# The first pair of heads through GpSimd's casting queue, and the last tile stored in two transfers per queue

## The chip, the core and the metric

The kernel runs on one core of a Trainium2 chip. The metric is the device time of one execution in microseconds (us); for the kernel before it is 431.96, the median of three runs (430.53 to 432.34). The profile is of one execution of the same program, and its span, from the first to the last instruction, is 430.6 us. Engines are called as in the profile: PE is TensorE's matmuls, PEld its weight loads, DVE is VectorE, ACT is ScalarE, POOL is GpSimd, SP is SyncE. A "q" behind an engine's name is its instruction sequencer, which among other things issues transfers.

## What is computed

Attention with a squared ReLU in place of the softmax, for 8 batches of 12 heads, 448 positions and 64 channels a head; its output, with the heads side by side, goes through a gated feed-forward block (768 to 1536 and back).

```python
def _attn_ref(q, k, v):                      # q, k, v: (8, 12, 448, 64) fp32
    scores = scale * np.matmul(q, k.transpose(0, 1, 3, 2))
    attn = np.maximum(scores, 0.0) ** 2 / S
    return np.matmul(attn, v)

def _moe_ref(x, w_gate, w_val, w_out):       # x: (3584, 768), d_ff = 1536
    g = x @ w_gate
    gelu = 0.5 * g * (1.0 + erf(g * inv_sqrt2))
    val = x @ w_val
    return (gelu * val @ w_out)              # (3584, 768) fp32
```

## The kernel before

All matmuls are in bf16. The inputs are fp32, so nearly all loads are issued on GpSimd's queue, whose transfers cast on the way. The kernel makes a list of operations for each engine, estimates when each could start, and emits them in that order (`run_plan`). Where it expects TensorE to wait within the first 30 us, it puts dummy matmuls (`fill`, on a tile of zeros named `warm`), so that the engine stays busy.

The beginning: a warm-up of dummy matmuls, then for each pair of heads of batch 0 the transposes of q and k on TensorE, a copy of them out of PSUM by VectorE, the scores (TensorE), the ReLU (ScalarE), the square (VectorE), and the product with v (TensorE, `add_values`).

```python
warm_op = Op("PE0", 3.8, lambda: emit_warm_up())
...
def emit_warm_up():
    t = new_bank(None)
    for _ in range(9):
        for j in range(2):
            nc.tensor.matmul(t[HALF[j], :], warm[:, HALF[j]], warm[:, :],
                             start=True, stop=True, tile_position=(0, P * j))
```

The first two heads of batch 0 are loaded in another way than the rest: SyncE issues two fp32 transfers, one for q and one for k, into a tile `first`. VectorE then rounds the first head of both to bf16, and ScalarE the second.

```python
def load_first():
    first = const.tile([128, 2, SC * D], f32)
    got = []
    for i, src in enumerate((q, k)):
        op = Op("SP", 0.0, lambda i=i, src=src: nc.sync.dma_start(
            first[HALF[i], :, :], src[0, 0:2].rearrange("h (p c) d -> p h (c d)", c=SC)), prio=-1)
        ...
    def emit(j):
        ...
        if j:
            nc.scalar.copy(o, first[:, j, :])
        else:
            nc.vector.tensor_copy(o, first[:, j, :])
...
got = load_first()
for h0, h1 in ((2, 4), (4, 8), (8, 12)):
    load_qk(0, 0, h0, h1)            # GpSimd's queue, casting
    load_qk(0, 1, h0, h1)
    if h0 == 2:
        POOL[0].after = got[1]
        POOL.append(Op("POOL", 0.6, lambda: make_identity(nc, ident)))
    if h0 > 2:
        load_v(0, h0 - 4, h1 - 4)
```

The transposes of a pair, and the place in the order that its product with v is given (`step` is the planned time of one unit of scores):

```python
for c in range(SC):                          # 7 chunks x 2 heads = 14 transposes a pair
    for j in range(2):
        nc.tensor.transpose(t[HALF[j], c, :], src[:, 2 * (2 * m + r) + j, c, :],
                            ident[:, :], tile_position=(0, P * j))
...
x = lo + u * step + max(4.5, (3.2 + 2 * (pr == 0) if b == 0 else 2.5) * step)
```

The end: the output is made in tiles of 128 rows (two chunks of 64) and in column groups, 0 to 383 and 384 to 767. The last tile has three groups, 0 to 383, 384 to 575 and 576 to 767, so that the last piece is small. Each group has 24 pairs of matmuls, then a copy out of PSUM, which VectorE does for the last tile. In the last tile each group is stored as soon as it is copied: one half of the rows by SyncE's queue and the other half by ScalarE's.

```python
bounds = (0, OGS, OGS + OGS // 2, 2 * OGS) if last else (0, OGS, 2 * OGS)   # OGS = 384
cols = slice(bounds[g], bounds[g + 1])
...
cp = Op("DVE" if last else "ACT", 0.48, emit_copy, [ops[1][-1]], prio=1)
if last:
    SP.append(Op("SP", 0.6, lambda: emit_store(0, nc.sync, cols), [cp], prio=-1))
    ACT.append(Op("ACT", 0.1, lambda: emit_store(1, nc.scalar, cols), [cp], prio=-1))
elif g == NG - 1:
    SP.extend(Op("SP", 0.6, lambda j=j: emit_store(j, nc.sync, slice(0, d_model)), [cp], prio=-1)
              for j in range(2))
```

Of the kernel before, what the change touches and what calls it, by code (L numbers as in the profile page):

```python
# [88 lines left out]
def kernel(  # L89
# [10 lines left out]
    nc = tc.nc  # L100
    f32 = mybir.dt.float32
    bf16 = mybir.dt.bfloat16
# [3 lines left out]
    B, H, S, D = q.shape  # L106
    P = 64
    SC = S // P
# [10 lines left out]
    NG = 2  # L119
# [9 lines left out]
    const = ctx.enter_context(tc.tile_pool(name="const", bufs=1))  # L129
    wpool = ctx.enter_context(tc.tile_pool(name="wpool", bufs=1))  # L130
    qkv = ctx.enter_context(tc.tile_pool(name="qkv", bufs=2))
# [21 lines left out]
    HALF = (slice(0, P), slice(P, 2 * P))  # L153
# [4 lines left out]
    def mm(o, lhsT, rhs, row, col, start, stop):  # L158
        return nc.tensor.matmul(o, lhsT, rhs, start=start, stop=stop,  # L159
                                tile_position=(P * row, P * col))  # L160

    def wait_lower(box):

        tc.add_manual_dep(nc.tensor.reg_mov(n_reg, 0).ins, box[1].ins.name, SYNC, reason="bank")

    ACT, DVE, POOL, SP, IDLE = [], [], [], [], []
    arrivals = {}
# [6 lines left out]
    w12_op, wo_op, head_op = {}, {}, {}  # L174
    qk16, v16 = {}, {}
# [38 lines left out]
        for pr in range(h0 // 2, h1 // 2):  # L214
            head_op[b, pr, i] = op

    def load_first():

        first = const.tile([128, 2, SC * D], f32)
        got = []  # L220
        for i, src in enumerate((q, k)):
            op = Op("SP", 0.0, lambda i=i, src=src: nc.sync.dma_start(  # L222
                first[HALF[i], :, :], src[0, 0:2].rearrange("h (p c) d -> p h (c d)", c=SC)), prio=-1)
            arrivals[op] = 2 * 4 * S * D / 300e3
            SP.append(op)
            got.append(op)

        def emit(j):
            if 0 not in qk16:
                qk16[0] = qkv.tile([128, H * S // P * D], bf16, name="qk16", tag="qk16")  # L230
            o = qk16[0].rearrange("p (h x) -> p h x", h=H)[:, j, :]
            if j:
                nc.scalar.copy(o, first[:, j, :])
            else:
                nc.vector.tensor_copy(o, first[:, j, :])  # L235

        ops = [Op("DVE", 0.5, lambda: emit(0), got, lag=0.1), Op("ACT", 0.5, lambda: emit(1), got, lag=0.1)]
        DVE.append(ops[0])
        ACT.append(ops[1])
        head_op[0, 0, 0], head_op[0, 0, 1] = ops  # L240
        return got

    def load_v(b, h0, h1, deps=()):

        for i in range(2):
            def emit(i=i):
                if b not in v16:
                    v16[b] = qkv.tile([128, H, VC, D], bf16, name="v16", tag="v16")
                c0 = i * (SC - VC)
                return nc.gpsimd.dma_start(  # L250
                    v16[b][HALF[i], h0:h1, :, :],
                    v[b, h0:h1].rearrange("h (p c) d -> p h c d", c=SC)[:, :, c0:c0 + VC, :])
            op = load(4 * (h1 - h0) * VC * P * D, emit, deps, rate=400e3 if b else 300e3)
            for pr in range(h0 // 2, h1 // 2):
                head_op[b, pr, 2 + i] = op
# [50 lines left out]

    bank_of = {}
    lower, pairs = [], []
    warm_op = Op("PE0", 3.8, lambda: emit_warm_up())
    ring = [warm_op]  # L310

    in_bank = []

    def new_bank(reader, shape=(128, 512), dtype=f32):
        in_bank.append(reader)
        return psF.tile(list(shape), dtype, name="ff", tag="F")
# [15 lines left out]
    def ring_dep():  # L332
        return [ring[-FB]] if len(ring) >= FB else []
# [7 lines left out]
    def then(at, step, los, his, done):  # L341

        for i, lo in enumerate(los):
            lower.append((at[i] if isinstance(at, list) else at + i * step, lo))
        pairs.append(("then", los[-1], his))
        bank_of[los[-1]] = done
# [209 lines left out]
    def add_out(at, t, g):  # L556

        box = {}
        last = 2 * t + 2 == B * SC
        bounds = (0, OGS, OGS + OGS // 2, 2 * OGS) if last else (0, OGS, 2 * OGS)  # L560
        cols = slice(bounds[g], bounds[g + 1])
        N = bounds[g + 1] - bounds[g]
        step = RS * N / OGS
        chunks = [divmod(2 * t + j, SC) for j in range(2)]

        def emit(r, fc):
            if not box:
                box[0] = new_bank(cp)
            i, o = divmod(fc, WOG)
            if r == 1 and fc == 0:  # L570
                wait_lower(box)
            for j, (b, c) in enumerate(chunks):
                ins = mm(box[0][HALF[j], 0:N], uT[b][HALF[r], fc, c * P:(c + 1) * P],
                         wo[i][HALF[r], o, cols], r, j, r == 0 and fc == 0,
                         r == 1 and fc == FC - 1)
            box[1] = ins

        def emit_copy():
            if g == 0:
                osb[t] = opool.tile([TT, d_model], f32, name="osb", tag="osb")  # L580
            (nc.vector.tensor_copy if last else nc.scalar.copy)(osb[t][:, cols], box[0][:, 0:N])  # L581

        def emit_store(j, engine, cols):
            b, c = chunks[j]
            rows = out[b * S:(b + 1) * S, :].rearrange("(p c) d -> c p d", c=SC)
            engine.dma_start(rows[c, :, cols], osb[t][HALF[j], cols])

        ops = [[Op(f"PE{r}", step, lambda r=r, fc=fc: emit(r, fc),
                   [wo_op[fc // WOG], *(u_op[b, fc] for b, _ in chunks),
                    *(ring_dep() if r == 0 and fc == 0 else ())], lag=0.24)  # L590
                for fc in range(FC)] for r in range(2)]

        cp = Op("DVE" if last else "ACT", 0.48, emit_copy, [ops[1][-1]], prio=1)
        ring.append(cp)
        (DVE if last else ACT).append(cp)
        if last:
            SP.append(Op("SP", 0.6, lambda: emit_store(0, nc.sync, cols), [cp], prio=-1))
            ACT.append(Op("ACT", 0.1, lambda: emit_store(1, nc.scalar, cols), [cp], prio=-1))
        elif g == NG - 1:
            SP.extend(Op("SP", 0.6, lambda j=j: emit_store(j, nc.sync, slice(0, d_model)), [cp], prio=-1)  # L600
                      for j in range(2))
        then(at, step, *ops, cp)


    got = load_first()
    for h0, h1 in ((2, 4), (4, 8), (8, 12)):
        load_qk(0, 0, h0, h1)
        load_qk(0, 1, h0, h1)
        if h0 == 2:
            POOL[0].after = got[1]  # L610
            POOL.append(Op("POOL", 0.6, lambda: make_identity(nc, ident)))
        if h0 > 2:
            load_v(0, h0 - 4, h1 - 4)
# [42 lines left out]
    for b in range(B):  # L656
        if b == 0:
            lo, hi = -60.0, -12.0
        elif b == 1:
            lo, hi = LO1, starts[1] - LEAD  # L660
        elif b == 2:
            lo, hi = starts[1] + 6.0, starts[2] - LEAD
        else:
            lo, hi = starts[b - 1] - LEAD, starts[b] - LEAD
        step = (hi - lo) / NU
        if b < EARLY:
            for m in range(NM):
                for rs in ((0,), (1,)) if b == 0 else ((0, 1),):

                    x = (1.5 * step if rs == (1,) else -3.0) if b == 0 else -5.0 if m else -2.0  # L670
                    work.append((lo + SC * m * step + x, 1, add_transposes, (b, m, rs)))
        for pr in range(NPAIR):
            u = SC * (pr // 2) + (VC - 1, SC - 1)[pr % 2]
            x = lo + u * step + max(4.5, (3.2 + 2 * (pr == 0) if b == 0 else 2.5) * step)
            work.append((PLACE5 if (b, pr) == (0, NPAIR - 1) else x, 2, add_values, (b, pr)))
        for u in range(NU):
            work.append((lo + u * step, 3, add_scores, (b, u)))
# [17 lines left out]
    PE0 = [op for _, op in lower]  # L695
# [24 lines left out]

    def emit_warm_up():
        t = new_bank(None)
        for _ in range(9):
            for j in range(2):
                nc.tensor.matmul(t[HALF[j], :], warm[:, HALF[j]], warm[:, :],
                                 start=True, stop=True, tile_position=(0, P * j))
# [34 lines left out]
```

## Time and profile before

| | us |
|---|---|
| median of three runs | 431.96 (430.53 to 432.34) |
| span of the profiled execution | 430.6 |
| TensorE matmuls busy | 420.6 (98% of the span), 9,089 recorded |
| weight loads busy | 358.6 (83%) |
| ScalarE busy | 224.3 (52%) |
| VectorE busy | 213.8 (50%) |
| GpSimd busy | 70.6 (16%) |

A matmul counts as busy from its start to a modelled end, and matmuls overlap, so 98% does not say that TensorE runs at its peak. It does say that it is nearly never without work, dummy matmuls included. "Granted clock" is the share of TensorE's full clock that the chip gives it; over the whole span it is 0.99. A wait in the profile is an engine's idle time, with the instruction or transfer that ended it. A transfer has a time of issue, in which the sequencer or GpSimd prepares it, and a time of landing, at which its semaphore says that all of it has arrived; "us to landing" counts from the start of the issue.

### The profile page before, as it was taken

The numbers are of one execution on the slowest core, as the hardware profiler recorded it, in microseconds if no ns is written. First come the engines' busy times: TensorE is split into PE (matmuls) and PEld (weight loads), VectorE is DVE, ScalarE is ACT, GpSimd is POOL, SyncE is SP. The second block draws the span as 40 slices with busy tenths as digits, with TensorE's granted clock in tenths as the row PEclk, the third lists the DMA queues.
The fourth block names the chain that finished last, engine by engine and source line by source line (L and its number), as shares of the span: only waits on it lengthen the run. The fifth ranks groups of instructions, "written<-read, shape, count | busy, mean of one in ns | idle before, by whom it ended". The sixth has DMA issues, their size and how long they took to land.

```text
span 430.6 us, 19602 instructions
## 1 busy us (share of the span) xinstructions
PE 420.6 (98%) x9089; PEld 358.6 (83%) x9092; DVE 213.8 (50%) x348; ACT 224.3 (52%) x321; POOL 70.6 (16%) x114
## 2 busy tenths in 40 slices
PE   6999999999999999999999999999999999999995
PEld 2456678879998888979999978979999988977895
DVE  1884676257644566355643565455643555212201
ACT  2963774276666555555556555555546555322220
POOL 8654420012200122011300023011310000000000
PEclk8999999999999999999999999999999999999998
DMA  9999999987994399644965369645984100120034
GB/s 154 196 198 199 202 207 140 164 97 96 128 128 92 37 114 132 121 82 70 137 107 126 52 77 149 126 77 58 129 146 97 38 4 3 47 68 3 2 76 113
DMA packets 75377, 45.14 MB, mean 105 GB/s; under 512 B 36128, under 2 KB 71840, under 8 KB 75296
## 3 DMA queue, kind: packets, MB, share of 16 engines
q0 software_dynamic: 36800, 24.16, 41.8%
q1 hardware_dynamic: 38256, 19.54, 25.2%
q8 instruction: 71, 1.16, 1.1%
q10 hardware_dynamic: 240, 0.20, 0.2%
q14 instruction: 10, 0.08, 0.1%
HBM read 48.76 MB, written 11.01 MB: 139 GB/s over the span
## 4 chain that ended last, share of the span: by engine, by line
PE 96%; DMA 1%; ACT 1%; issue 0%; SPq 0%; DVE 0%; DVEq 0%
PE ff L159 86%; PE sp L159 8%; PE ff L330 1%; DMA first<-in_k_dram 1%; PE ff L368 1%; PE sp L368 1%; ACT rl L415 1%; SPq L222 0%; DVE qk L235 0%; DVE osb L581 0%; DVEq L235 0%
## 5 line engine op out<-in xcount | busy, mean ns | idle before, releaser
L159 PE MATMUL ff<-xT,wg 64*64 64x448 bf16 x2304 | 216.8, 349 | 0.0
L159 PE MATMUL ff<-xT,wv 64*64 64x448 bf16 x2304 | 215.5, 349 | 0.0
L415 ACT ACTIVATE rl<-sp 128x896 bf16<-128x896 f32 x168 | 152.5, 917 | 91.7 <-PE sp L159 73.9
L159 PE MATMUL ff<-wo,uT 64*64 64x384 bf16 (+1 forms) x2736 | 150.9, 320 | 0.0
L159 PEld LDWEIGHTS <-wg 64*64 64x64 bf16 x2304 | 125.1, 107 | 17.4 <-issue 0.8
L159 PEld LDWEIGHTS <-wv 64*64 64x64 bf16 x2304 | 125.2, 107 | 16.8 <-issue 1.6
L421 DVE TENSOR_TENSOR attnT<-rl 128x896 bf16<-128x896 bf16 x168 | 104.0, 623 | 69.2 <-ACT rl L415 68.0
L159 PEld LDWEIGHTS <-uT 64*64 64x64 bf16 x2736 | 127.0, 107 | 4.2
L159 PE MATMUL sp<-qkT 64*64 64x448 bf16 (+1 forms) x768 | 106.9, 330 | 1.2 <-ACT rl L415 0.9
L529 DVE TENSOR_TENSOR uT<-gel,ff 128x448 bf16<-128x448 bf16 x96 | 59.5, 620 | 79.0 <-PE ff L159 66.0
L159 PE MATMUL ff<-attnT,v 64*64 64x448 bf16 (+1 forms) x768 | 84.9, 326 | 0.1
L524 ACT ACTIVATE gel<-ff 128x448 bf16<-128x448 f32 x96 | 52.1, 543 | 55.3 <-PE ff L159 54.8
L159 PEld LDWEIGHTS <-qkT 64*64 64x64 bf16 x768 | 43.0, 107 | 11.2 <-issue 4.9
L159 PEld LDWEIGHTS <-v 64*64 64x64 bf16 x768 | 45.6, 107 | 5.2 <-issue 1.1
L581 ACT COPY osb<-ff 128x384 f32<-128x384 f32 x54 | 25.7, 477 | 45.9 <-PE ff L159 43.2
L474 DVE TENSOR_SCALAR xT<-ff 128x448 bf16<-128x448 f32 x48 | 29.9, 624 | 31.2 <-PE ff L159 31.2
L211 POOL DMA_DIRECT2D qk<-in_q_dram x24 | 14.9, 623 | 133.6 <-DVE uT L529 125.8
L250 POOL DMA_DIRECT2D v<-in_v_dram x44 | 27.4, 627 | 40.1 <-DVE uT L529 32.0
L211 POOL DMA_DIRECT2D qk<-in_k_dram x24 | 14.8, 616 | 64.4 <-DVE uT L529 55.6
L284 DVE COPY qkr<-qk 128x1792 bf16<-128x1792 bf16 x18 | 19.3, 1078 | 0.0
L368 PEld LDWEIGHTS <-qk 128*64 128x64 bf16 x168 | 5.5, 115 | 6.6 <-DVE qk L235 3.1
L581 DVE COPY osb<-ff 128x192 f32<-128x192 f32 (+1 forms) x3 | 1.2, 421 | 18.3 <-PE ff L159 18.3
(25 smaller groups left out, 44.7 us busy)
## 6 DMA issues: line engine op xcount, KB each, us to landing
out_dram<-osb SPq DMA_DIRECT2D x54, 192.0 KB, 2.9
v<-in_v_dram POOLq DMA_DIRECT2D x42, 128.0 KB, 4.3
qk<-in_q_dram POOLq DMA_DIRECT2D x23, 224.0 KB, 4.2
qk<-in_k_dram POOLq DMA_DIRECT2D x23, 224.0 KB, 4.8
wg<-in_moe_w_gate_dram POOLq DMA_DIRECT2D x6, 384.0 KB, 10.7
wv<-in_moe_w_val_dram POOLq DMA_DIRECT2D x6, 384.0 KB, 11.6
wo<-in_moe_w_out_dram POOLq DMA_DIRECT2D x4, 576.0 KB, 14.9
v<-in_v_dram POOLq DMA_DIRECT2D x2, 384.0 KB, 10.6
```

The source lines that it names most:

```text
L159: return nc.tensor.matmul(o, lhsT, rhs, start=start, stop=stop, tile_position=(P * row, P * col))
L211: op = load(4 * (h1 - h0) * S * D, lambda: nc.gpsimd.dma_start(tile_of().rearrange("p (h x) -> p h x", h=H)[:, h0:h1, :], src[b, h0:h1].re ...
L250: return nc.gpsimd.dma_start(v16[b][HALF[i], h0:h1, :, :], v[b, h0:h1].rearrange("h (p c) d -> p h c d", c=SC)[:, :, c0:c0 + VC, :])
L284: nc.vector.tensor_copy(qkr[b][:, m], qk16[b].rearrange("p (h c d) -> p c h d", c=SC, d=D)[:, :, 4 * m:4 * m + 4])
L330: nc.tensor.matmul(t[:, :], warm[:, 0:128], warm[:, :], start=True, stop=True)
L368: nc.tensor.transpose(t[HALF[j], c, :], src[:, 2 * (2 * m + r) + j, c, :], ident[:, :], tile_position=(0, P * j))
L415: nc.scalar.activation(rl[:, :, :], box[0][:, :, 0:S], AF.Relu)
L421: nc.vector.tensor_tensor(a[:, :, :], box[1][:, :, :], box[1][:, :, :], op=ALU.mult)
L474: nc.vector.tensor_scalar_mul(xT[b][:, pr, :], box[0][:, 0:S], scalar1=out_scale)
L524: nc.scalar.activation(gel[b, fc][:, :], box[0][:, 0:S], AF.Gelu)
L529: u_op[b, fc].ins = nc.vector.tensor_tensor(uT[b][:, fc, :], gel.pop((b, fc))[:, :], box[0][:, 0:S], op=ALU.mult).ins
L581: (nc.vector.tensor_copy if last else nc.scalar.copy)(osb[t][:, cols], box[0][:, 0:N])
```

## The change

The special load of the first pair goes. Heads 0 and 1 are loaded like all others, by GpSimd's casting queue, ahead of heads 2 and 3; SyncE's two fp32 loads and the two roundings are gone, and the order of loads behind them stays. The warm-up is ten rounds in place of nine, and the first pair's product with v is placed two units of scores earlier, as the other pairs' is. In the last tile, the second column group is no longer stored by itself: when the third is copied, one transfer per queue stores both (384 columns). The number of stores at the end falls from three to two per queue. What the change is for: less work at the start on VectorE, ScalarE and SyncE's queue, and a shorter row of transfers behind the last matmul.

```diff
-    def load_first():
-
-        first = const.tile([128, 2, SC * D], f32)
-        got = []
-        for i, src in enumerate((q, k)):
-            op = Op("SP", 0.0, lambda i=i, src=src: nc.sync.dma_start(
-                first[HALF[i], :, :], src[0, 0:2].rearrange("h (p c) d -> p h (c d)", c=SC)), prio=-1)
-            arrivals[op] = 2 * 4 * S * D / 300e3
-            SP.append(op)
-            got.append(op)
 ... (the rounding of the two heads, on DVE and ACT, goes with it)
-    warm_op = Op("PE0", 3.8, lambda: emit_warm_up())
+    warm_op = Op("PE0", 4.3, lambda: emit_warm_up())
 ...
-        if last:
-            SP.append(Op("SP", 0.6, lambda: emit_store(0, nc.sync, cols), [cp], prio=-1))
-            ACT.append(Op("ACT", 0.1, lambda: emit_store(1, nc.scalar, cols), [cp], prio=-1))
-        elif g == NG - 1:
+        if last and g != 1:
+
+            part = slice(bounds[g and g - 1], bounds[g + 1])
+            SP.append(Op("SP", 0.6, lambda: emit_store(0, nc.sync, part), [cp], prio=-1))
+            ACT.append(Op("ACT", 0.1, lambda: emit_store(1, nc.scalar, part), [cp], prio=-1))
+        elif g == NG - 1 and not last:
 ...
-    got = load_first()
-    for h0, h1 in ((2, 4), (4, 8), (8, 12)):
+    for h0, h1 in ((0, 2), (2, 4), (4, 8), (8, 12)):
         load_qk(0, 0, h0, h1)
         load_qk(0, 1, h0, h1)
-        if h0 == 2:
-            POOL[0].after = got[1]
+        if h0 == 0:
             POOL.append(Op("POOL", 0.6, lambda: make_identity(nc, ident)))
 ...
-            x = lo + u * step + max(4.5, (3.2 + 2 * (pr == 0) if b == 0 else 2.5) * step)
+            x = lo + u * step + max(4.5, (3.2 if b == 0 else 2.5) * step)
 ...
-        for _ in range(9):
+        for _ in range(10):
```

More of the change, by code (lines that the diff above doesn't have):

```diff
@@ L215, in load_qk @@
             head_op[b, pr, i] = op
-    def load_first():
-        first = const.tile([128, 2, SC * D], f32)
-        got = []
-        for i, src in enumerate((q, k)):
-            op = Op("SP", 0.0, lambda i=i, src=src: nc.sync.dma_start(
-                first[HALF[i], :, :], src[0, 0:2].rearrange("h (p c) d -> p h (c d)", c=SC)), prio=-1)
-            arrivals[op] = 2 * 4 * S * D / 300e3
-            SP.append(op)
-            got.append(op)
[L228 to L241, printed above, removed]
     def load_v(b, h0, h1, deps=()):
```

## The prediction

> **What bounds the kernel now.** I read the page first (shares, chain), then the busy times of six stretches that I cut myself, then the chain in order of time for the first 30 us, the timelines of TensorE and ScalarE there, the DMA issues, and the timeline of the last 6 us. The page's chain says whose kernel this is:
>
> ```profile
> span 430.6 us, 19602 instructions
> PE 96%; DMA 1%; ACT 1%; issue 0%; SPq 0%; DVE 0%; DVEq 0%
> ```
>
> TensorE holds 96% of the path to the end. So only what TensorE does not fill with needed work can be won or lost, and the stretches say where that is:
>
> ```profile
> core 0: us, PE busy (x) PEld busy (x) DVE busy (x) ACT busy (x) POOL busy (x), PEclk, DMA share, GB/s
> 1.00:4.70 3.70, 3.51 (x18) 1.36 (x18) 0.15 (x2) 1.22 (x2) 3.38 (x7) 1.00 0.66 149
> 4.70:7.35 2.65, 0.01 (x2) 0.00 (x0) 0.39 (x1) 0.46 (x1) 2.65 (x5) 1.00 1.15 187
> 7.35:10.42 3.07, 3.07 (x25) 1.28 (x25) 0.62 (x1) 0.11 (x1) 2.46 (x5) 0.52 1.27 177
> 10.42:29.00 18.58, 17.09 (x257) 8.98 (x257) 16.14 (x29) 17.54 (x21) 10.68 (x16) 0.99 1.39 197
> 29.00:426.02 397.02, 396.90 (x8797) 346.96 (x8796) 195.99 (x315) 204.74 (x298) 51.19 (x80) 1.00 0.65 99
> 426.02:430.60 4.58, 0.00 (x0) 0.00 (x0) 0.36 (x1) 0.00 (x0) 0.00 (x0) 0.64 0.33 88
> ```
>
> From 29 to 426 TensorE is idle for 0.12 us: nothing in there is touched by the change. The change acts on two ends: the first 10.42 us, up to the first ReLU, and the last 4.58 us. Between 10.42 and 29 ScalarE is the bound (17.54 of 18.58 us busy, its 21 ReLUs of about 0.84 us pitch), and TensorE is padded with dummy matmuls. A stage bound by ScalarE simply starts earlier when its first ReLU does. The chain of the opening says what sets that:
>
> ```profile
> 0.74 0.77 SPq L222
> 1.56 5.24 DMA first<-in_k_dram
> ...
> 6.91 0.40 DVE qk L235
> ...
> 7.35 1.11 PE ff L368 x14
> 8.46 1.39 PE ff L330 x3
> 9.85 0.89 PE sp L159 x6
> ```
>
> K's fp32 load is issued at 1.56 and lands at 1.56 + 5.24 = 6.80; the rounding ends at 7.31; the transposes start at 7.35. TensorE, whose warm-up ended at 4.70, has been idle for 2.65 us, and in the next stretch its granted clock is 0.52: the 14 transposes take 1.11 us here, against 0.58 for the same 14 at 14.45.
>
> **What the skill says.** (1) "DMA: Bandwidth & Descriptors", section Queues, rings and completion order: each DMA engine takes turns between the queue rows that have work. The trace agrees: four loads on two queues share the engines from 2 to 6 us, and in each queue the second is late:
>
> ```profile
> first<-in_q_dram SPq DMA_DIRECT2D x1, 224.0 KB, 3.5
> first<-in_k_dram SPq DMA_DIRECT2D x1, 224.0 KB, 5.2
> qk<-in_q_dram POOLq DMA_DIRECT2D x1, 112.0 KB, 3.6
> qk<-in_k_dram POOLq DMA_DIRECT2D x1, 112.0 KB, 5.1
> out_dram<-osb SPq DMA_DIRECT2D x1, 96.0 KB, 2.1
> out_dram<-osb ACTq DMA_DIRECT2D x1, 96.0 KB, 2.4
> out_dram<-osb SPq DMA_DIRECT2D x2, 48.0 KB, 2.0
> out_dram<-osb ACTq DMA_DIRECT2D x2, 48.0 KB, 2.1
> ```
>
> (2) The same page, SWDGE vs HWDGE vs iDMA: a transfer that casts must be issued by GpSimd, which is why the first pair needed a rounding step once SyncE loaded it. (3) The same page, Anatomy of one DMA: some 2 us of a transfer are fixed, the rest is bytes. The last four lines agree: twice the bytes cost 0.1 to 0.3 us more on a 2.0 us base. (4) "TensorE: Matmul & The Clock Gate", Part 1: the clock is halved after an idle window of 3.4 us, and that window runs free of the kernel's start. The trace shows a halved clock after the idle stretch; in which phase another execution falls, it can't show.
>
> **Part 1, the opening.** Removed: two fp32 loads on SyncE's queue and two roundings (0.39 on VectorE, 0.56 on ScalarE, side by side). Added: two loads of 112 KB at the head of GpSimd's queue, which now cast on the way. GpSimd's first issue starts at 1.25 and its second at 1.95 now, with heads 2 and 3; in the changed kernel heads 0 and 1 get these two places. How long do they take there? Today's first takes 3.6 us and its second 5.1 us, with 448 KB of fp32 on the other queue in their way. With that gone: in the stretch from 6 to 7 us, where GpSimd's queue has the engines to itself, it finished 226 packets, and these two loads have 128 each (64 partitions, two heads), 0.57 us apiece. Later single loads of this queue land in 3.1 us (V, 128 KB) to 3.4 us (Q, 224 KB). I take 3.3 us for K: 1.95 + 3.3 = 5.25, and no rounding. The ten rounds of warm-up: nine end at 4.70, the tenth adds 0.2 to 0.4 (by the clock), so TensorE is free at 4.9 to 5.1 and idles for a few tenths at most. The transposes start at about 5.3 in place of 7.35: 2.05 us.
>
> From there to the first ReLU it takes 3.07 us today at the half clock. At the full one: transposes 0.58, VectorE's copy 0.62 and two handovers of 0.05 each, then from scores to ReLU 0.44 (16.24 to 16.68 later on), about 1.75 us in all; the three dummy matmuls (0.66) fit under the copy. So 1.3 us can be won on top. I count on 0.9: with no idle stretch the halving has no cause, but the warm-up itself ran slowly (18 matmuls side by side in pairs in 3.51 us, 0.39 a pair, while a dummy of 512 columns has a pitch of 0.22 at full speed and 0.45 in the slow stretch), so the moment at which the clock opens can still fall behind 5.3. First ReLU at about 7.5 in place of 10.42: **2.9 us**.
>
> Does the stage behind it move as far? Three things could hold it. Loads: TensorE first reads V at 16.64, which landed by 10.47; the first gate weights at 28.99, landed at 17.7; the second block at 36.5, landed at 25.4; the third at 43.4, landed at 31.7; the last output weights at 71.0, landed at 63.2. All have 6 us or more in hand. GpSimd's queue gains 256 packets (1.1 us) at its front, and loses the rival that took about as much of the engines. Order: the instruction order of the two programs differs in 215 of 9,095 matmuls, all before 30 us; the first pair's value matmuls stand two score units earlier, and would be reached about 4.9 us after the first ReLU, at 12.4, when their V is there. ScalarE: same 21 ReLUs. I take the 2.9 us as carried whole to the end.
>
> **Part 2, the end.** Last matmul 426.01, last copy done 426.40. Today SyncE and ScalarE each issue three stores: ScalarE's at 425.77, 426.42 (0.73 long) and 427.25, and the third, issued 0.85 us after its data were ready, lands 1.96 later at 429.21; the closing of the program takes the rest to 430.6. In the changed kernel the second issue waits for the last copy (426.4) and moves 96 KB: 426.43 + 2.4 = 428.83. That is **0.4 us** (0.3 to 0.6).
>
> Sum: 431.96 - 2.9 - 0.4 = 428.7 us.
>
> **The rivals.** (a) *The load is no faster through GpSimd.* If the first two software loads keep today's 3.6 and 5.1 us, K lands at 7.05, the transposes start at 7.1, TensorE still idles for 2 us at the same clock, and all that is left is 0.2 + 0.4: 431.3. For it: those are the only two loads issued this early, and someone built the fp32 path, which must have looked quicker once. Against it: their rival is the very thing that goes away. (b) *The clock stays at half speed* up to the first ReLU by an unlucky window: 2.05 + 0.4, so 429.5. (c) *The start moves and something behind takes it back*: the earlier value matmuls hold TensorE[...] while scores wait behind them, and ScalarE gets gaps beyond the 0.9 us it has now. A gap of 1 us gives 429.7. Against: the margin of some 2 us for V. (d) *Second transposes late*: heads 2 and 3 now go third and fourth in the queue, issued at 3.10 and 3.72. At 3.3 to 3.6 us they land by 7.3, and are wanted at about 7.5; half a microsecond at worst.
>
> **Range and chances.** The three runs of before spread over 1.8 us, as the clock's window and the two queues' turns would make them. Full success (3.5 us + 0.6) gives 427.7, rival (a) 431.3 or somewhat less. So 427.4 to 431.2. A change of 2% is 8.6 us; the whole opening and end have hardly that much idle. Faster by over 2%: 0.01; within: 0.98; slower by over 2%: 0.01.
>
> **What would show it.** Right: K of the first pair lands before 5.7; TensorE has no idle stretch over 0.6 us before 10; the clock is full from about 6; first ReLU between 6.9 and 8.3; gate matmuls begin near 26; from last matmul to end about 4.2 in place of 4.6. Wrong: K at 6.5 or later (rival a); a clock of 0.5 with no idle time ahead of it (b); ReLUs with new gaps before 26 while TensorE stands at a value matmul (c); a last store that lands 2.8 us after its issue.

## The result, and the profile after

The changed kernel takes 429.0 us (median; 428.47 to 429.34), beside 432.15 for the kernel before: a ratio of 0.9935, 95% interval 0.9915 to 0.9955. The prediction was 428.7 in a range of 427.4 to 431.2.

The page of the changed kernel, the same two lines as before:

```profile
span 427.4 us, 19594 instructions
PE 98%; ACT 0%; issue 0%; DVE 0%; ACTq 0%
```

The transfer that held 1% of the path is gone from it. The busy times of the opening, in the stretches used for the kernel before (span, then busy time of PE, PEld, DVE, ACT, POOL, then clock, DMA share and GB/s):

```profile
1.00:4.70 3.70, 3.51 (x18) 1.52 (x20) 0.14 (x2) 1.22 (x2) 3.38 (x7) 1.00 0.53 65
4.70:7.35 2.65, 2.65 (x28) 1.34 (x27) 0.62 (x1) 0.00 (x0) 2.65 (x6) 1.00 1.00 130
7.35:10.42 3.07, 2.91 (x42) 1.18 (x35) 1.97 (x4) 2.85 (x4) 2.33 (x5) 1.00 1.15 154
```

From 4.70 to 7.35, where TensorE had stood idle, it is busy throughout. The clock's column needs care: it shows 1.00 also where the trace has no clock record yet. Here the first record begins at 6.42, and the pace tells what came before. The chain in order of time:

```profile
1.19 4.48 PE ff L699 x19
5.67 0.75 PE ff L342 x14
6.41 0.77 PE ff L304 x3
7.18 0.53 PE sp L159 x8
```

Ten rounds of warm-up take 4.48 us, one per 0.43 us by their weight loads: the half clock, up to its end. The loads themselves:

```profile
qk<-in_q_dram POOLq DMA_DIRECT2D x2, 112.0 KB, 3.2
qk<-in_k_dram POOLq DMA_DIRECT2D x2, 112.0 KB, 3.2
...
out_dram<-osb SPq DMA_DIRECT2D x2, 96.0 KB, 2.2
out_dram<-osb ACTq DMA_DIRECT2D x2, 96.0 KB, 2.5
```

K of the first pair is issued at 1.95 and lands at 4.89 (2.94 us), the transposes start at 5.46. From there ScalarE's timeline (start, length, and in brackets the idle time ahead):

```profile
7.57 5.78 ACT L389 ACTIVATE rl<-sp 128x896 bf16<-128x896 f32 x7 [5.34 <-PE sp L159]
13.70 5.01 ACT L389 ACTIVATE rl<-sp 128x896 bf16<-128x896 f32 x6 [0.36 <-PE sp L159]
19.10 6.89 ACT L389 ACTIVATE rl<-sp 128x896 bf16<-128x896 f32 x8 [0.38 <-PE ff L159]
```

Where the two profiles stand against each other, mark by mark:

| us from the span's start | before | after | earlier by |
|---|---|---|---|
| K of heads 0, 1 landed | 6.81 | 4.89 | 1.92 |
| first transposes | 7.35 | 5.46 | 1.89 |
| first ReLU | 10.42 | 7.57 | 2.85 |
| last of batch 0's 21 ReLUs ends | 29.18 | 25.99 | 3.19 |
| first gate matmul | 28.99 | 25.81 | 3.18 |
| last matmul ends | 426.01 | 423.36 | 2.65 |
| last store landed | 429.21 | 426.30 | 2.91 |
| end of the span | 430.56 | 427.40 | 3.16 |

So 2.9 us come from before the first ReLU. Of these, 1.9 lie before the transposes, and 1.0 on the way from transposes to ReLU (3.07 before, 2.11 after). Between the first gate matmul and the last matmul 0.53 us are given back. Behind the last matmul 0.51 us are won: half of it up to the last landing, half between that and the end of the span.

### The profile page after: what moved, and what is told of

The parts are those of the page before. It is cut to its first block, busy times and chain, and to the rows that moved or that the text cites. A ratio compares the mean times of both kernels' runs of the same rounds, so it can differ in the third digit from the quotient of the medians.

```text
span 427.4 us, 19594 instructions
## 1 busy us (share of the span) xinstructions
PE 421.1 (99%) x9090; PEld 359.7 (84%) x9093; DVE 213.1 (50%) x347; ACT 223.5 (52%) x320; POOL 71.5 (17%) x116
## 4 chain that ended last, share of the span: by engine, by line
PE 98%; ACT 0%; issue 0%; DVE 0%; ACTq 0%
PE ff L159 86%; PE sp L159 8%; PE ff L304 1%; PE ff L699 1%; PE sp L342 1%; PE ff L342 1%; ACT rl L389 0%; DVE osb L555 0%; DVE warm L145 0%; DVE table L148 0%; ACTq L389 0%
## 5 line engine op out<-in xcount | busy, mean ns | idle before, releaser
L159 PEld LDWEIGHTS <-wg 64*64 64x64 bf16 x2304 | 126.9, 107 | 17.3 <-issue 0.9
L159 PEld LDWEIGHTS <-wv 64*64 64x64 bf16 x2304 | 126.8, 107 | 17.3 <-issue 2.1
L159 PEld LDWEIGHTS <-uT 64*64 64x64 bf16 x2736 | 128.7, 107 | 3.9
L159 PE MATMUL sp<-qkT 64*64 64x448 bf16 (+1 forms) x768 | 108.3, 328 | 0.5 <-ACT rl L389 0.4
L159 PE MATMUL ff<-attnT,v 64*64 64x448 bf16 (+1 forms) x768 | 86.2, 326 | 0.1
L159 PEld LDWEIGHTS <-qkT 64*64 64x64 bf16 x768 | 44.1, 106 | 9.8 <-issue 4.2
L159 PEld LDWEIGHTS <-v 64*64 64x64 bf16 x768 | 46.7, 107 | 5.4 <-issue 1.3
```

## The experiments

A ratio is to the kernel before on the same chip, with its 95% interval. Its medians were 431.55 us (the first four), 431.3 (the next four) and 431.57 (the last four).

**The stores alone.** The kernel before with the last hunk of stores.

```diff
-        if last:
+        if last and g != 1:
+            part = slice(bounds[g and g - 1], bounds[g + 1])
```

> The kernel before with the new stores alone. My theory: from the last matmul to the end 4.55 us become 4.05, because the third store of ScalarE's queue is no longer issued 0.85 us after its data; time 0.5 us under the kernel before, about 431.6. Rival (the last landing is set by the bytes of all stores together, not by the row of issues): less than 0.2 us.

Measured: 431.06 us, ratio 0.9985 (0.9972 to 0.9998), which is 0.65 us with an interval of 0.1 to 1.2. In the profile the last store lands 2.91 us after the last matmul; before it was 3.21. The span then closes 0.97 us after this landing, before 1.35. What SyncE does from the last landing on says why (count of its semaphore instructions, ns of one, first and last start; before, and in this run):

```profile
L756 SPq EVENT_SEMAPHORE  x10: 17/28/28, 429.2 to 430.5; - x10
L758 SPq EVENT_SEMAPHORE  x4: 17/22/28, 428.4 to 429.3; - x4
```

At its end the program lets SyncE check the transfers' semaphores one after the other, about 0.06 us each. In the kernel before the store that lands last stands early in that row, so that seven checks still follow it; here only one does. Six fewer make the 0.38 us. Which place the last store gets belongs to the program and not to the execution: the closing took 1.34 to 1.36 us in all three profiles with the fp32 path and three stores per queue, 0.97 in both with that path and two, 0.99 with the changed opening and three (the next run) and 1.10 in the changed kernel. So the profile gives the stores 0.3 us of landing and, in this kernel, 0.38 of closing; the time agrees with the sum.

**The opening alone.** The changed kernel with the three old stores per queue.

> The changed kernel with the three stores of before. My theory: the two parts add, so 2.6 us under the kernel before, 0.5 over the changed kernel: about 429.5, first ReLU at 7.5 to 8. Rival (the parts share the gain, because the span is set by transfers in both): 429.0 as the changed kernel.

Measured: 428.98 us, ratio 0.9949 (0.9926 to 0.9972), first ReLU at 7.33. That is 2.2 us (1.2 to 3.2) of the kernel before; with the 0.65 of the stores it gives 2.85, close to the 2.8 of the whole change (0.65% of 432). The intervals are too wide to test the sum to half a microsecond. I had expected 0.5 us over the changed kernel, and the median is level with its 429.0, the figure of the rival. The profiles lie between: from the last matmul to the end it takes 4.18 us here, 4.04 in the changed kernel, because the new stores win 0.26 us of landing there and lose 0.12 of closing.

**The rival put back.** The changed kernel, and beside it SyncE's two fp32 loads into a tile that nothing reads.

```diff
+    first = const.tile([128, 2, SC * D], f32)
+    for i, src in enumerate((q, k)):
+        SP.append(Op("SP", 0.0, lambda i=i, src=src: nc.sync.dma_start(
+            first[HALF[i], :, :], src[0, 0:2].rearrange("h (p c) d -> p h (c d)", c=SC)), prio=-1))
```

> The changed kernel, and beside it SyncE's two fp32 loads of before, which nothing reads. If the rival on the other queue is what made the first loads slow (my theory): K of heads 0 and 1 lands near 7.0 in place of 4.9, TensorE idles from 5.6 to 7, its clock drops again, and the time rises by 1.5 to 2.7 us, to 430.5 to 431.7. If GpSimd's casting path is quicker in itself and the rival does little: K lands by 5.5 and the time stays within 0.3 us of 429.0.

Measured: 429.94 us, ratio 0.9973 (0.996 to 0.9986). Its issues and TensorE's timeline:

```profile
qk<-in_q_dram POOLq DMA_DIRECT2D x1, 112.0 KB, 3.7
qk<-in_k_dram POOLq DMA_DIRECT2D x1, 112.0 KB, 4.7
```

```profile
1.19 4.48 PE L703 MATMUL ff<-warm 128*64 128x512 bf16 x20 [1.19 <-DVE table L148]
6.77 0.96 PE L342 MATMUL ff<-ident,qk 128*64 128x128 bf16 x14 [1.10 <-DMA qk<-in_k_dram]
7.66 1.46 PE L304 MATMUL ff<-warm 128*128 128x512 bf16 x3
```

K now takes 4.7 us in place of 2.94 and lands at 6.63; TensorE waits 1.10 us for it, and runs the first transposes (0.96) and dummies (1.46 for three) at half speed. The first ReLU comes at 9.70. In landing the other queue costs 1.7 us, where I expected 2.1. In time the medians say 0.9 us over the changed kernel's 429.0, the two ratios (0.9973 and 0.9935) 1.6; I had expected 1.5 to 2.7. The profiled execution, at 431.35, was one of the slower ones of this run.

**The warm-up stretched in the kernel before.** Nothing but the count of rounds.

```diff
-        for _ in range(9):
+        for _ in range(15):
```

> The kernel before with 15 rounds of warm-up in place of 9, so that TensorE stays busy until K's fp32 load lands. K still lands near 6.8 and the transposes start at 7.35 to 7.6. If the half clock costs what I put it at: first ReLU at 9.1 to 9.4 in place of 10.42, time 1.1 us less, about 431.0. If arrival is all that counts and the clock is worth nothing: first ReLU stays at 10.4 and the time at 432.1 or a little above.

Measured: 429.72 us, ratio 0.9962 (0.9949 to 0.9976): 1.6 us (1.0 to 2.2), more than I expected, from twelve dummy matmuls. Its timeline:

```profile
1.19 5.91 PE L725 MATMUL ff<-warm 128*64 128x512 bf16 x30 [1.19 <-DVE table L148]
6.93 0.55 PE L368 MATMUL ff<-ident,qk 128*64 128x128 bf16 x14
7.42 0.82 PE L330 MATMUL ff<-warm 128*128 128x512 bf16 x3
```

The transposes take 0.55 us for the 1.11 of before, and the first ReLU comes at 8.65, that is 1.72 after them in place of 3.07. K landed at 5.80 here, not 6.81; in the run with the stores alone at 5.99. So the profile of before that I had read showed a late landing, and the arrival that can usually be won is smaller than it looked. The run with the stores alone has nearly the same landing with nine rounds, and so shows the clock by itself: its transposes start earlier than here (6.54 for 6.93), and its first ReLU still comes 0.96 us later (9.61). The padding also narrows the spread: its 13 executions lie between 429.27 and 430.26, the 52 of the kernel before between 429.48 and 433.26. It takes the long executions away; the shortest ones stay about where they were.

**The fp32 loads by themselves.** The kernel before, with GpSimd's first load held until K's fp32 load has landed (the identity is made ahead of it).

```diff
-        load_qk(0, 0, h0, h1)
+        load_qk(0, 0, h0, h1, [got[1]] if h0 == 2 else ())
```

> The kernel before, but GpSimd's first load (heads 2 and 3) waits until K's fp32 load has landed, so that the two fp32 loads have the DMA engines to themselves. If the two queues hindered each other (my theory): K lands at 4.5 to 5.0 in place of 6.8, rounding ends by 5.6, first ReLU at about 7.5; heads 2 and 3 come at 8 to 8.7, which may hold the second transposes by up to 1 us; time 429.5 to 430.5. If the fp32 path is slow in itself: K still at 6 or later, everything behind it later too, time above 432.5.

Measured: 431.98 us, ratio 1.0019 (1.0007 to 1.0032), slower. The two loads alone:

```profile
first<-in_q_dram SPq DMA_DIRECT2D x1, 224.0 KB, 3.7
first<-in_k_dram SPq DMA_DIRECT2D x1, 224.0 KB, 3.8
```

K lands at 5.32, the transposes start at 5.86 and the first ReLU at 7.75: the landing as this theory has it, if later than I said. But heads 2 and 3 now come at 9.5, K of heads 4 to 7 at 14.34, and ScalarE gets gaps of 1.11, 1.90 and 1.42 us ahead of its 3rd, 7th and 8th ReLU. What the opening wins, the loads behind it lose. The profiled execution was the longest of the 22 (434.47), so its gaps may be larger than usual: its clock was halved once more, from 14.64 to 18.06, after waits for these loads. TensorE's idle time ahead of the first transposes, 0.97 us, halved nothing here: the clock had opened at 4.40 and stayed open. The run also splits the gain in arrival: even without a rival the fp32 way has its data, rounded, ready for TensorE at 5.86; GpSimd's way has it at 4.89.

**The place of the first pair's values.** The changed kernel with `3.2 + 2 * (pr == 0)` put back.

> The changed kernel with the first pair's product with v where the kernel before had it, two units of scores later. My theory: the place is worth nothing, because ScalarE's ReLUs bound this stage in either order: within 0.3 us of the changed kernel. Rival: the earlier place is what let the stage run its 21 ReLUs in 18.42 us in place of 18.76: then 0.3 us or more slower.

Measured: 429.05 us, ratio 0.9954 (0.9938 to 0.997). The stage's 21 ReLUs take 18.58 us from first to last here, 18.42 in the changed kernel, 18.76 before. The times are level with the changed kernel's: no worth of the place shows in them. The profiles hint at a small one: where neither the clock nor a load disturbs the stage, it took 18.57 to 18.59 us in the three with the old place (this one and the two with 15 rounds) and 18.35 to 18.44 in five with the new. Of the 0.34 us between the first two profiles, then, some 0.1 to 0.2 would be the place; the rest may lie in the slow clock, which before reached past the first ReLU (to 10.86).

**A shorter warm-up in the changed kernel.** Eight rounds, since K lands at 4.89 and the transposes wait for the warm-up's end.

> The changed kernel with 8 rounds of warm-up in place of 10. In the changed kernel's profile K lands at 4.89, but the warm-up holds TensorE until 5.46 or so. If arrival now stands behind the warm-up (my theory): transposes at 4.95 to 5.05, first ReLU at 7.1 to 7.3, and up to 0.5 us less, 428.5. Rival (the shorter warm-up opens the clock later, or leaves an idle gap that halves it): no gain or a loss of up to 1 us.

Measured: 429.95 us, ratio 0.9972 (0.9955 to 0.9989), with single executions from 428.96 to 431.99. In the profile the transposes start at 5.21, but the clock opens at 6.89 and the first ReLU comes at 7.66, no earlier. The rival's figure came true, no gain or a loss; its reason isn't shown. The transposes did run slowly (0.96 us), but the changed kernel's own profiles with ten rounds have the clock open at 6.42 and, in a later run, at 6.94. K landed at 5.08 here, so that TensorE waited 0.40 us for it.

**The last stores cut elsewhere.** 576 and 192 columns in place of 384 and 384.

```diff
-        if last and g != 1:
+        if last and g:
-            part = slice(bounds[g and g - 1], bounds[g + 1])
+            part = slice(bounds[g] if g > 1 else 0, bounds[g + 1])
```

> The changed kernel with the last tile's stores cut elsewhere: columns 0 to 575 when the second group is copied, 576 to 767 at the end, two transfers per queue as in the changed kernel, but the last moves 48 KB in place of 96 KB. My theory (landing is a fixed 2 us plus bytes): last landing 2.1 us after its issue in place of 2.5, 0.2 to 0.4 us less than the changed kernel. Rival (the earlier 144 KB store is still on the engines, and holds the last one): no gain.

Measured: 429.48 us, ratio 0.9956 (0.9941 to 0.9972). The issues at the end:

```profile
out_dram<-osb SPq DMA_DIRECT2D x1, 144.0 KB, 2.4
out_dram<-osb ACTq DMA_DIRECT2D x1, 144.0 KB, 2.8
out_dram<-osb SPq DMA_DIRECT2D x1, 48.0 KB, 2.5
out_dram<-osb ACTq DMA_DIRECT2D x1, 48.0 KB, 2.6
```

The 48 KB stores take as long as the 96 KB ones did (2.2 and 2.5), though in the kernel before 48 KB landed in 2.0: half the bytes won nothing behind a larger store. The last lands 3.26 us after the last matmul, 0.3 later than in the changed kernel. Nearly all of that is a later issue: ScalarE is still busy with the 144 KB issue and starts the last one 0.69 us after the last matmul, in the changed kernel 0.43. My theory of a fixed time plus bytes missed both.

By chance this execution had its clock open at 4.49, and its first ReLU at 6.75, 0.8 us before the changed kernel's. It won nothing by it, and one line of TensorE's timeline says why:

```profile
11.44 0.58 PE L342 MATMUL ff<-ident,qk 128*64 128x128 bf16 x14 [0.37 <-DMA qk<-in_k_dram]
```

The third transposes wait for K of heads 4 to 7, which landed at 11.30, and the last of the 21 ReLUs ends at 25.95, against 25.99 in the changed kernel. There these transposes start at 11.47 and K landed at 11.34. The opening has reached its next bound.

**The changed kernel again**, as a reference for the last three.

> The changed kernel itself, beside the next three on the same chip, so that they can be compared with it: 428.5 to 429.5, 2.3 to 2.8 us under the kernel before. In its profile the third transposes (heads 4 and 5) start within 0.2 us of the landing of K of heads 4 to 7, or wait for it.

Measured: 428.9 us, ratio 0.9933 (0.9909 to 0.9956). The second point missed: in this execution K of heads 4 to 7 landed at 10.83, and the third transposes started at 11.65 without waiting for it. The first ReLU was at 7.81 here. How near that bound is depends on the execution.

**The identity made later**, so that the loads of heads 2 and 3 follow the first two at once.

```diff
-        if h0 == 0:
+        if h0 == 2:
             POOL.append(Op("POOL", 0.6, lambda: make_identity(nc, ident)))
```

> The changed kernel, but GpSimd makes the identity after it has issued the loads of heads 2 and 3, not before. If the gap of half a microsecond that the identity leaves in the row of issues delays the loads behind it (my theory): heads 2 and 3 land 0.4 to 0.6 us earlier, K of heads 4 to 7 by 10.9, and where the clock opens early the time falls by up to 0.5 us; where it opens late ScalarE bounds and nothing changes. Mean 0.1 to 0.4 us under the changed kernel. Rival (the first microseconds of the queue are slow for another reason, the engines' own): K of heads 4 to 7 still at 11.1 to 11.4, no gain.

Measured: 429.68 us, ratio 0.9956 (0.9943 to 0.9968): no gain. The two loads are issued 0.54 us earlier and land only 0.1 to 0.3 earlier (6.26 and 6.97 for 6.55 and 7.10), K of the first pair even later (5.39 for 4.89), and K of heads 4 to 7 at 10.87. That last landing is the one I forecast, but the changed kernel beside it had 10.83. The edit only moves the gap behind heads 2 and 3; the loads of heads 4 to 7 are issued when they were (4.29 for 4.26). So for heads 2 and 3 most of the earlier issue is lost again on the way, and the gap ahead of them is not what makes them slow; for heads 4 to 7 this run tests nothing.

**A short warm-up with an idle stretch.** The changed kernel with 5 rounds.

> The changed kernel with 5 rounds of warm-up in place of 10: the loads are untouched, TensorE is idle from 3.3 until K lands near 5. If the half clock is a cost of its own, apart from arrival (my theory): transposes at 5.0 but 3.0 us from there to the first ReLU, so 8.0 to 8.2 in place of 7.57, the whole stage up to 1 us later, time 0.4 to 1.2 us over the changed kernel. If arrival alone counts: as fast as the changed kernel or 0.4 us faster.

Measured: 430.08 us, ratio 0.9962 (0.9949 to 0.9974), 1.2 us over the changed kernel beside it.

```profile
1.19 2.35 PE L699 MATMUL ff<-warm 128*64 128x512 bf16 x10 [1.19 <-DVE table L148]
5.00 0.96 PE L342 MATMUL ff<-ident,qk 128*64 128x128 bf16 x14 [1.46 <-DMA qk<-in_k_dram]
5.89 1.46 PE L304 MATMUL ff<-warm 128*128 128x512 bf16 x3
7.28 0.96 PE L159 MATMUL sp<-qkT 64*64 64x448 bf16 x8
```

Nothing is later in arrival, and the transposes start 0.46 us earlier than in the changed kernel. But all of it runs at half pace until 11.26, where the trace's first clock record begins: 2.92 us to the first ReLU (7.92), then idle stretches of 0.59 and 0.43 us between the next ones, and the stage ends at 27.68 in place of 26.16. Here the idle time ahead of the data cost more than the wait itself.

**The kernel before, with padding and the new stores.** 15 rounds, two stores per queue, and still the fp32 path.

> The kernel before with two edits only: 15 rounds of warm-up and the two stores per queue at the end. The fp32 path stays. If the changed kernel's gain is mostly the clock and the stores, and the way of loading little (what the run with 15 rounds suggests): 429.0 to 429.5, level with the changed kernel within 0.4 us. If GpSimd's path has a gain of its own of a microsecond: 429.8 or more.

Measured: 429.32 us, ratio 0.9944 (0.9923 to 0.9965). Its stretches from the first transposes to the first ReLU, and from there to the first gate matmul:

```profile
7.05:8.77 1.72, 1.72 (x27) 0.75 (x23) 0.62 (x1) 0.00 (x1) 1.57 (x3) 1.00 1.33 182
8.77:27.16 18.39, 17.47 (x257) 8.93 (x254) 16.14 (x29) 17.42 (x21) 11.16 (x16) 1.00 1.39 198
```

From transposes to first ReLU 1.72 us again. With the old way of loading, this version is level with the changed kernel (0.9933, 0.9909 to 0.9956): what remains for GpSimd's path in time is 0.4 us between the medians, which the intervals don't separate. No version tried is faster than the changed kernel beyond the spread.

## Why the prediction was right, and where it was not

The time was right and the mechanism named was at work: the two ends, the clock, the row of stores. That the sum came out so near, 3.3 us predicted and 2.8 by the ratio (1.9 to 3.7), is in part luck. The profile it started from had an unusually late K (6.81; 5.80 to 5.99 in three later profiles of that path), which put the arrival too high; and the padding alone, without the new load, later gave 1.6 us, more than the 0.9 set down for the clock. The two errors ran against each other. Step by step:

- *The load through GpSimd is faster once its rival is gone: 5.25 for K.* Right, 4.89. Putting the rival back gave 6.63. Rival (a) fell.
- *The transposes start at about 5.3.* 5.46, but for another reason. "TensorE is free at 4.9 to 5.1" was wrong: I let the clock open during the warm-up as it had at 4.03 before, and here it opened at 6.42, so ten rounds lasted to 5.67. The warm-up now ends after the data. The prediction's own warning, that the clock could open behind 5.3, came true.
- *2.05 us of arrival and 0.9 of clock.* Between the two profiles, 1.89 and 0.96, as said. As causes they can't be split like that. TensorE's idle time before was both the late arrival and the cause of the half clock, and filling it with dummies, on the old way of loading, gave 1.6 us. The 1.75 us worked out for the way from transposes to ReLU at full clock were right: 1.72 to 1.73 in three profiles with an open clock. Left out was that the slow clock reached past the first ReLU, to 10.86.
- *All loads have 6 us or more in hand.* The list left out K of heads 4 to 7. In the kernel before it landed at 8.76 for transposes at 14.45; in the changed kernel at 11.34 for 11.47. At the 226 packets per us that I had read from 6 to 7 us, the 1,024 packets up to its end, from about 3.6 on, would be through near 8.1 (an estimate). In the stretch from 4.70 to 7.35 the changed kernel moved 130 GB/s, the kernel before 187, of which GpSimd's queue alone some 170. It cost nothing at a first ReLU of 7.57, and took all of one at 6.75. Why the queue is slow there stays open; the run with the identity made later did not cure it.
- *The 2.9 us are carried whole to the end.* They were 3.18 at the first gate matmul and 2.65 after the last one. No matmul waits in that stretch, in either profile, and the one wait of a weight load for a transfer (0.4 us, gate weights) stands in both; the loss lies in steps of about 0.1 us between 42 and 80 us. In the two padded runs of the fp32 path the same stretch took 396.4 us, and it varied up to 398.0 over all profiles, so I can't put a cause to it.
- *The end: 0.4 us.* The last landing moved 0.3 us closer to the last matmul. The profile's total of 0.51 holds another 0.25 from the closing, which the prediction took as unchanged: SyncE has four semaphores to check after the last landing in place of eight. The fixed 2 us of point (3) are given by the Trainium skill ("DMA: Bandwidth & Descriptors", Anatomy of one DMA) for transfers that GpSimd issues. For these stores of SyncE and ScalarE only the trace speaks, with 2.0 to 2.1 us for 48 KB and 2.1 to 2.4 for 96 KB.
- *The rivals.* (b) came half true: the clock was slow up to 6.42 with no idle time ahead of it. (c) fell: ScalarE's gaps are 0.36 and 0.38 us, 0.36 and 0.55 before. (d) fell: heads 2 and 3 had landed by 7.10, and the second transposes start at 7.64. A slip that nothing hangs on: the full success is 427.9 by its own terms, not 427.7.

## What to carry to other kernels

An idle TensorE ahead of its first data cost twice here: the wait, and then a slow clock for several microseconds (once, with the clock already open, 0.97 us of it halved nothing). Before work goes into an earlier arrival, stretch the warm-up until the data are there; here that alone gave 1.6 us (1.0 to 2.2), where the whole change gave 2.8. The second queue did not help the one piece that everything waited for (K landed 4.7 us after its issue with it, 2.9 without): give that piece the engines first and ask then which load is waited for next. And the start of one profile is one draw: compare several before splitting a microsecond into causes.

## What the runs showed of the hardware

- A cast load of 112 KB on GpSimd's queue landed 2.9 to 3.4 us after its issue (K of the first pair, in eight profiles), while the fp32 load of the same heads on SyncE's queue, without the other queue, took 3.8 us. With both queues busy these became 4.3 to 5.1 and 4.2 to 5.2.
- The half clock at the start ended at very different times in nearly the same warm-up: between 4.03 and 6.94 in eight profiles with nine or ten rounds and no idle time ahead of the mark. In all 14 traces the marks at which the clock changes lie whole multiples of 3.41 us apart (4.03, 7.44, 10.86 in the kernel before; 4.40, 14.64, 18.06 with the fp32 loads by themselves), and where they fall differs between executions. The 3.41 us ahead of an opening were busy matmul time for 2.84 us in the kernel before, 3.01 with eight rounds, and 3.21 or more in the others. It stayed half after up to 2.51 us (the rival put back, up to 6.58), and once after 2.85 (five rounds, 4.44 to 7.85). Ahead of the two halvings during the work it was 0.76 and 1.59 us; after 2.44 (fp32 loads by themselves, 4.40 to 7.81) it stayed open. So in these runs the cost of an idle stretch depends on how it falls between the marks. The ends of matmuls are modelled, so these are rough.
- A 48 KB store issued behind a 144 KB one took 2.5 to 2.6 us in place of 2.0.
